# PSUM score tiles by half of a query tile, first loads over two queues, and more sigmoid groups, in a fused attention and feed-forward kernel

## The chip, the core and the metric

The kernel runs on one core of a Trainium2 chip. The metric is the time of one execution on the device, in microseconds (us). Each time is a median of three to nine executions of the same build.

The names in the profile are PE for TensorE's matmuls, PEld for its weight loads, DVE for VectorE, ACT for ScalarE, POOL for GpSimd and SP for the engine that issues most loads. L326 is line 326 of the kernel in question. Inserted lines shift the numbers, so the same instruction is L326 before, L335 after the change.

## The reference, cut to what matters

```python
# q, k, v: (8 batches, 8 heads, 576, 64); tau: scalar
scores = scale * np.matmul(q, k.transpose(0, 1, 3, 2))
thresh = np.max(scores, axis=-1, keepdims=True) - tau
scores = np.where(scores >= thresh, scores, -1000000000.0)
scores = scores - np.max(scores, axis=-1, keepdims=True)
attn = np.exp(scores)
attn = attn / (np.sum(attn, axis=-1, keepdims=True) + 1e-09)
attn_out = np.matmul(attn, v)
# x: attn_out as (4608, 512); w_gate, w_val: (512, 1536); w_out: (1536, 512)
g = x @ w_gate
silu = g * (1.0 / (1.0 + np.exp(-g)))
out = (silu * (x @ w_val)) @ w_out
```

## The kernel before: the parts that the argument touches

The order of instructions on each engine is fixed when the kernel is built. Attention for one batch is interleaved with the feed-forward products of the batch before it, which fill TensorE while the softmax goes through the other engines.

**A score block.** One block serves two heads and two half tiles of 64 queries each. It has 16 matmul calls, and each f32 call appears as two matmuls in the trace, so a full block reads as x32. Its result fills two PSUM tiles, and the pool has just two, so each block needs the tiles of the block before.

```python
ps_s = ctx.enter_context(tc.tile_pool(name="ps_s", bufs=2, space=bass.MemoryType.PSUM))
...
put = [(pss[h], u, h, q0 + u * D) for u in range(2) for h in range(2)] if t < NT else \
    [(pss[0], h, h, q0) for h in range(2)]
for x in range(0, len(put), 2):
    for g in range(NG):
        a, c = divmod(g, 2)
        for ps, u, h, col in put[x:x + 2]:          # two heads in turn: both PSUM tiles
            hs = heads[h]
            nc.tensor.matmul(ps[g * G:(g + 1) * G, u, 0:SH], qT[hs, col + a * G:col + (a + 1) * G],
                             kT[hs, c * SH:(c + 1) * SH], start=True, stop=True)   # L286
...
for x, tile_ in enumerate(pss):                     # one maximum for each PSUM tile, L306
    nc.vector.tensor_reduce(out=mx[:, 2 * x:2 * x + 2, 0], in_=tile_[:, :, 0:SH], axis=AX.X, op=ALU.max,
                            negate=True)
...
for x in range(m):                                  # four exponentials, L322
    nc.scalar.activation(ps[x], scs[x], AF.Exp, bias=nm[:, x:x + 1])
...
for x in range(m):                                  # four masking passes, L326; the last reader of the scores
    nc.vector.scalar_tensor_tensor(out=ps[x], in0=scs[x], scalar=th[:, x:x + 1], in1=ps[x],
                                   op0=ALU.is_ge, op1=ALU.mult, accum_out=sm[:, x, 0:1])
```

This is a ring: the scores free VectorE to take the maximum, then come exponentials and masking passes, and the masking passes free the PSUM tiles for the next block's scores. After the masking passes, ScalarE copies the row sums, VectorE takes their total and reciprocal, and GpSimd and ScalarE normalise the weights, which VectorE then transposes.

**First loads.** q and k go over SP's queue into one pair of places, so the second pair waits until the first is transposed; GpSimd scales q.

```python
raw = ld.tile([P, NJ, G], F32, name=f"{name}raw")
...
    nc.sync.dma_start(out=raw[g * G:(g + 1) * G], ...)                                    # L230
nc.gpsimd.tensor_scalar(out=raws[0], in0=raws[0], scalar1=scl, scalar2=None, op0=ALU.mult)  # L233
```

**Sigmoids.** ScalarE keeps the table of the exponential for attention, so sigmoids are collected in groups: a table load, the sigmoids, and a second load by a dummy exponential. The hidden tiles are then multiplied and, in most units, added up for a scheme with seven products instead of eight. A unit is a run of 256 tokens. Its last group takes three gate tiles, and at the last unit of a batch VectorE does its multiplications.

```python
def sigmoids(eng=None):
    eng = nc.vector if attended else eng or nc.gpsimd
    for hts, gt, own in unsig:
        nc.scalar.activation(gt, gt, AF.Sigmoid)                                          # L500
        for y, (x, ht) in enumerate(own):
            eng.tensor_tensor(out=ht, in0=ht, in1=gt[:, 2 * y:2 * y + 2, :], op=ALU.mult)   # L502
    if not attended:
        nc.scalar.activation(idle, tau_s, AF.Exp)                                         # L505
    ...                                             # three sums on eng for each pair, L513 to L515
...
if unsig:                                           # at the end of a unit
    sigmoids(nc.gpsimd if ready else nc.vector)
```

Of the kernel before, what the change touches and what calls it, by code (L numbers as in the profile page):

```python
# [10 lines left out]
F32 = mybir.dt.float32  # L11
U32 = mybir.dt.uint32
U64 = mybir.dt.uint64
AF = mybir.ActivationFunctionType
ALU = mybir.AluOpType
# [4 lines left out]
def kernel(  # L20
# [30 lines left out]
    nc = tc.nc  # L51
    P = 128
    B, H, S, D = q.shape
# [3 lines left out]
    NF = DFF // P  # L57
    G = 32
# [164 lines left out]
    def load_qk(i):  # L223
        b, hp_ = divmod(i, NP)
        raws = []
        for name, src, order in (("q", q, "(j r) (e d) -> e r j d"), ("k", k, "(j r) (e d) -> e r j d" if b == 0 else "(r j) (e d) -> e r j d")):
            raw = ld.tile([P, NJ, G], F32, name=f"{name}raw")
            for g in range(NG):
                h, e = divmod(g, 2)
                nc.sync.dma_start(out=raw[g * G:(g + 1) * G],  # L230
                                  in_=src[b, 2 * hp_ + h].rearrange(order, r=G, d=G)[e])
            raws.append(raw.rearrange("p j d -> p (j d)"))
        nc.gpsimd.tensor_scalar(out=raws[0], in0=raws[0], scalar1=scl, scalar2=None, op0=ALU.mult)  # L233
        return raws

    def load_v(seg):
# [29 lines left out]
    def scores(seg, t):  # L266
        qT, kT, tiles, halved = seg["qT"], seg["kT"], seg["tiles"], seg["halved"]
        if halved and "p" not in seg:
            seg["p"] = arenas[seg["i"] % 2]
        q0 = t * P - seg["q0"]  # L270
        heads = [slice(h * D, (h + 1) * D) for h in range(2)]
        if t < NT:
            pss = [ps_s.tile([P, 2, 512], F32, name="sc") for _ in range(2)]
            at = [t, NT + 1 + t]
        else:
            pss = [ps_s.tile([P, 2, 512], F32, name="sc")]
            at = [t]
        if halved:
            put = [(pss[h], u, h, q0 + u * D) for u in range(2) for h in range(2)] if t < NT else \
                [(pss[0], h, h, q0) for h in range(2)]  # L280
            for x in range(0, len(put), 2):
                for g in range(NG):
                    a, c = divmod(g, 2)
                    for ps, u, h, col in put[x:x + 2]:
                        hs = heads[h]
                        nc.tensor.matmul(ps[g * G:(g + 1) * G, u, 0:SH], qT[hs, col + a * G:col + (a + 1) * G],  # L286
                                         kT[hs, c * SH:(c + 1) * SH], start=True, stop=True)
        elif t < NT:
            for h, hs in enumerate(heads):
                for n in range(2):  # L290
                    nc.tensor.matmul(pss[h][:, n, 0:SH], qT[hs, q0:q0 + P], kT[hs, n * SH:(n + 1) * SH],
                                     start=True, stop=True)
        else:
            for n, h in ((0, 0), (1, 1), (1, 0), (0, 1)):
                hs = heads[h]
                nc.tensor.matmul(pss[0][hs, n, 0:SH], qT[hs, q0:q0 + D], kT[hs, n * SH:(n + 1) * SH],
                                 start=True, stop=True)
        mx, nm, th, ri = (stp.tile([P, 4, 2] if x == "mx" else [P, 4], F32, name=x) for x in ("mx", "nm", "th", "ri"))
        sm = sums[0]
        sums.rotate(1)  # L300
        if halved:
            m = 2 * len(at)
            scs = [ps[:, u, 0:SH] for ps in pss for u in range(2)]
            ps = [seg["p"][:, x, u * SH:(u + 1) * SH] for x in at for u in range(2)]
            for x, tile_ in enumerate(pss):
                nc.vector.tensor_reduce(out=mx[:, 2 * x:2 * x + 2, 0], in_=tile_[:, :, 0:SH], axis=AX.X, op=ALU.max,  # L306
                                        negate=True)
            meet(mx, m, largest)
            nc.vector.tensor_reduce(out=nm[:, 0:m], in_=mx[:, 0:m, :], axis=AX.X, op=ALU.min)  # L309
        else:  # L310
            m = len(at)
            scs = [ps[:, :, 0:SH] for ps in pss]
            ps = [pbufs[0][:, x, :].rearrange("p (n s) -> p n s", n=2) for x in range(m)]
            pbufs.rotate(1)
            for x in range(m):
                nc.vector.tensor_reduce(out=nm[:, x:x + 1], in_=scs[x], axis=AX.XY, op=ALU.max, negate=True)
        if halved:
            nc.scalar.activation(th[:, 0:m], nm[:, 0:m], AF.Identity, bias=cut, scale=-1.0)  # L318
        for x in range(m):
            if not halved:  # L320
                nc.scalar.activation(th[:, x:x + 1], nm[:, x:x + 1], AF.Identity, bias=cut, scale=-1.0)
            nc.scalar.activation(ps[x], scs[x], AF.Exp, bias=nm[:, x:x + 1])  # L322
        yield
        turn(1)
        for x in range(m):
            nc.vector.scalar_tensor_tensor(out=ps[x], in0=scs[x], scalar=th[:, x:x + 1], in1=ps[x],  # L326
                                           op0=ALU.is_ge, op1=ALU.mult, accum_out=sm[:, x, 0:1])
        tot = stp.tile([P, 4], F32, name="tot")
        if halved:
            yield  # L330
            meet(sm, m, same)
            yield
            nc.vector.tensor_reduce(out=tot[:, 0:m], in_=sm[:, 0:m, :], axis=AX.X, op=ALU.add)
        else:
            nc.vector.tensor_reduce(out=tot[:, 0:m], in_=sm[:, 0:m, 0:3:2], axis=AX.X, op=ALU.add)  # L335
        nc.vector.reciprocal(out=ri[:, 0:m], in_=tot[:, 0:m])  # L336
        if not halved:
            yield
        for x in range(m):
            if halved and not split and x % 2:  # L340
                nc.gpsimd.tensor_scalar(out=ps[x], in0=ps[x], scalar1=ri[:, x:x + 1], scalar2=None, op0=ALU.mult)  # L341
            else:
                nc.scalar.activation(ps[x], ps[x], AF.Copy, scale=ri[:, x:x + 1])  # L343
        if halved:
            unturned.append([seg["p"][:, x, :] for x in at])
        else:
            unflipped.append((seg, t, [p.rearrange("p n s -> p (n s)") for p in ps]))
            yield
        yield
# [144 lines left out]
            del xts[j]  # L494
        yield HCOST

    def sigmoids(eng=None):
        eng = nc.vector if attended else eng or nc.gpsimd
        for hts, gt, own in unsig:
            nc.scalar.activation(gt, gt, AF.Sigmoid)  # L500
            for y, (x, ht) in enumerate(own):
# [5 lines that stand above are left out]
            for x, ht in own:  # L507
                if hts["seven"] and x >= NF2 // 2:

                    x -= NF2 // 2  # L510
                    fs = slice(2 * x, 2 * x + 2)
                    h11, h21 = hts[x][:, :, 0:P], hts[x][:, :, P:2 * P]
                    eng.tensor_tensor(out=hs3[:, fs], in0=h11, in1=h21, op=ALU.subtract)  # L513
                    eng.tensor_tensor(out=h21, in0=h21, in1=ht[:, :, P:2 * P], op=ALU.add)
                    eng.tensor_tensor(out=hs2[:, fs], in0=h21, in1=h11, op=ALU.subtract)  # L515
        unsig.clear()
# [118 lines left out]
    def block():  # L635
        late, last = iter(()), None
        while True:
            if not ready:
                yield from late
                if not ready:  # L640
                    yield 0
                continue
            unit = ready.popleft()
            j, lo, hi = unit
            cs = slice(lo, hi)
            hts, gts = {"seven": unit not in (FIRST, SECOND)}, {}
            hidden[unit] = hts
            sums = sums_of_weights() if last == SECOND else iter(())
            for f in range(0, NF, GR):
                if f == EARLY:  # L650
                    yield from late
                yield from gate(j, cs, f, hts, gts)
                if f >= EARLY:
                    next(sums, 0)
                yield from value(j, cs, f, hts, gts)
            if unsig:

                sigmoids(nc.gpsimd if ready else nc.vector)
            late = outputs(unit)
            last = unit  # L660

# [101 lines left out]

    fetch_qk(0)
    prepare(segs[0])
    fetch_weights(1)
    fetch_qk(1)
    fetch_weights(1)
    load_v(segs[0])
    fetch_weights(2)  # L770
    prev = None
# [89 lines left out]
```

## Time and profile before

The time is 1612.3 us, the median of three runs (1610.49 to 1613.5). The profiled execution spans 1607.7 us.

| engine | busy us | share |
|---|---|---|
| TensorE | 1523.9 | 95% |
| VectorE | 1071.2 | 67% |
| ScalarE | 826.0 | 51% |
| GpSimd | 628.9 | 39% |

TensorE is the bound. Two groups of the page show the ring of waits between it and VectorE. The columns are line, engine, operation, output and input, sizes and count; then busy us and mean ns; then the idle time just before such instructions, and the releaser of most of it.

```profile
L286 PE MATMUL sc<-kT,qT 64*32 64x288 f32 x4032 | 181.5, 419 | 40.6 <-DVE pall L326 40.2
L306 DVE TENSOR_REDUCE mx<-sc 128x2 f32<-128x576 f32 x252 | 179.1, 748 | 46.2 <-PE sc L286 42.5
```

TensorE waits for VectorE's masking pass, and VectorE waits for TensorE's scores. A block's second matmul already writes the second PSUM tile, which comes free only with the fourth pass, and no tile is whole until the block's last matmuls.

### The profile page before, as it was taken

Reading aid. Unit: us, or ns where it says so; the run is one execution under the profiler, and the core shown is the slowest. Engines: PE = TensorE matmul, PEld = TensorE weight load, DVE = VectorE, ACT = ScalarE, POOL = GpSimd, SP = SyncE. Lnnn points to the kernel's source line nnn. Section 1 sums busy time; section 2 is a strip of 40 time slices with the busy share of each in tenths; the row PEclk is TensorE's granted clock in tenths of the full one; section 3 lists DMA queues with packets and bytes.
Section 4 is the critical chain, followed back from the end, with each engine's and each line's share of the span. In section 5 each row is a group of like instructions: output and inputs, shape, how many; then the busy total and the mean of one; then the engine's idle time right before and its main releaser. Section 6 shows DMA issues by size and latency. Waiting matters only on the chain.

```text
span 1607.7 us, 31245 instructions
## 1 busy us (share of the span) xinstructions
PE 1523.9 (95%) x11728; PEld 1145.3 (71%) x11728; DVE 1071.2 (67%) x3232; ACT 826.0 (51%) x2133; POOL 628.9 (39%) x613
## 2 busy tenths in 40 slices
PE   6999778899998999899999999999999999999998
PEld 4666554457676777677777777776777777788887
DVE  6887887777677777674777776767676777722212
ACT  5877656555554564544464646464556455611110
POOL 3555533327533253234344444445363535210010
PEclk9999899999999999999999999999999999999999
DMA  7541321111111111110211111101111110000000
GB/s 172 148 139 60 70 49 31 43 44 31 31 43 44 31 31 43 31 28 17 43 31 44 31 44 31 27 18 44 31 37 37 44 31 28 3 14 0 13 14 14
DMA packets 176422, 66.90 MB, mean 42 GB/s; under 512 B 159632, under 2 KB 159632, under 8 KB 176272
## 3 DMA queue, kind: packets, MB, share of 16 engines
q1 hardware_dynamic: 173328, 55.47, 15.6%
q0 software_dynamic: 2944, 9.44, 1.7%
q8 instruction: 93, 1.52, 0.4%
q14 instruction: 57, 0.47, 0.1%
HBM read 55.44 MB, written 9.44 MB: 40 GB/s over the span
## 4 chain that ended last, share of the span: by engine, by line
PE 77%; DVE 12%; ACT 6%; issue 2%; SPq 1%; POOL 1%; DMA 1%; DVEq 0%; POOLq 0%; ACTq 0%
PE pv L466 20%; PE pg L466 19%; PE po L575 18%; PE sc L286 9%; PE xa L423 8%; DVE pall L326 3%; DVE mx L306 2%; PE po L542 2%; DVE pall L356 2%; ACT pall L322 1%; DVE mx L261 1%; ACT gt L500 1%; ACT L500 1%; SPq L230 1%; ACT L505 1%
## 5 line engine op out<-in xcount | busy, mean ns | idle before, releaser
L466 PE MATMUL pv<-xall,wgv 128*128 128x256 f32 x1728 | 404.6, 385 | 1.9 <-ACT gt L482 1.9
L466 PE MATMUL pg<-xall,wgv 128*128 128x256 f32 x1728 | 403.1, 385 | 0.5 <-DVE xall L403 0.5
L466 PEld LDWEIGHTS pv<-xall,wgv 128*128 128x128 f32 x1728 | 327.7, 192 | 68.5 <-issue 21.2
L466 PEld LDWEIGHTS pg<-xall,wgv 128*128 128x128 f32 x1728 | 325.6, 191 | 69.1 <-issue 17.2
L341 POOL TENSOR_SCALAR pall<-pall,ri 128x288 f32<-128x288 f32 x243 | 241.0, 1002 | 320.2 <-DVE ri L336 279.0
L326 DVE SCALAR_TENSOR_TENSOR pall<-sc,th,pall 128x288 f32<-128x288 f32 (+1 forms) x540 | 258.0, 528 | 45.0 <-ACT pall L322 44.2
L322 ACT ACTIVATE pall<-sc,nm 128x288 f32<-128x288 f32 (+1 forms) x540 | 236.7, 511 | 0.6
L286 PE MATMUL sc<-kT,qT 64*32 64x288 f32 x4032 | 181.5, 419 | 40.6 <-DVE pall L326 40.2
L306 DVE TENSOR_REDUCE mx<-sc 128x2 f32<-128x576 f32 x252 | 179.1, 748 | 46.2 <-PE sc L286 42.5
L343 ACT ACTIVATE pall<-pall,ri 128x288 f32<-128x288 f32 (+1 forms) x297 | 152.9, 560 | 92.0 <-DVE ri L336 91.0
L356 DVE STREAM_TRANSPOSE pall<-pall 128x576 f32<-128x576 f32 x252 | 181.4, 754 | 3.3 <-POOL pall L341 3.3
L264 ACT COPY sums<-sums 32x4 f32<-32x4 f32 (+1 forms) x560 | 108.5, 194 | 139.3 <-DVE pall L326 129.8
L575 PE MATMUL po<-wo,ht 128*128 128x256 f32 x768 | 176.6, 382 | 0.0
L318 ACT ACTIVATE th<-nm,cut 128x4 f32<-128x4 f32 (+1 forms) x140 | 41.4, 296 | 248.0 <-DVE nm L309 248.0
L575 PEld LDWEIGHTS po<-wo,ht 128*128 128x128 f32 x768 | 144.8, 190 | 27.9 <-issue 4.6
L286 PEld LDWEIGHTS sc<-kT,qT 64*32 64x32 f32 x4032 | 72.1, 107 | 125.7 <-issue 101.8
L489 DVE TENSOR_TENSOR ht<-gt,pv 128x512 f32<-128x512 f32 x102 | 69.8, 684 | 135.4 <-PE pv L466 120.1
L502 POOL TENSOR_TENSOR ht<-ht,gt 128x512 f32<-128x512 f32 x72 | 89.6, 1271 | 167.2 <-ACT gt L500 167.2
L423 PE MATMUL xa<-pall,vall 64*64 64x288 f32 x2016 | 131.9, 410 | 6.7 <-issue 6.7
L423 PEld LDWEIGHTS xa<-pall,vall 64*64 64x64 f32 x2016 | 80.9, 135 | 53.7 <-issue 14.2
L588 POOL TENSOR_TENSOR ht<-ht,xall 128x256 f32<-128x256 f32 x48 | 34.8, 727 | 211.1 <-PE po L575 208.3
L482 ACT COPY gt<-pg 128x512 f32<-128x512 f32 x108 | 63.5, 588 | 79.2 <-PE pg L466 78.5
(100 smaller groups left out, 1482.3 us busy)
## 6 DMA issues: line engine op xcount, KB each, us to landing
vall<-in_v_dram SPq DMA_DIRECT2D x112, 144.0 KB, 3.4
qraw<-in_q_dram SPq DMA_DIRECT2D x128, 72.0 KB, 2.5
kraw<-in_k_dram SPq DMA_DIRECT2D x128, 72.0 KB, 2.9
out_dram<-ob POOLq DMA_DIRECT2D x32, 256.0 KB, 2.5
wo<-in_moe_w_gate_dram SPq DMA_DIRECT2D x16, 384.0 KB, 3.6
wo<-in_moe_w_val_dram SPq DMA_DIRECT2D x16, 384.0 KB, 4.1
xall<-in_moe_w_out_dram SPq DMA_DIRECT2D x6, 768.0 KB, 4.6
wo<-in_moe_w_out_dram SPq DMA_DIRECT2D x2, 768.0 KB, 4.4
```

Source lines behind the costliest of these rows:

```text
L264: nc.scalar.copy(out, in_[:, :, 0])
L286: nc.tensor.matmul(ps[g * G:(g + 1) * G, u, 0:SH], qT[hs, col + a * G:col + (a + 1) * G], kT[hs, c * SH:(c + 1) * SH], start=True, stop=True)
L306: nc.vector.tensor_reduce(out=mx[:, 2 * x:2 * x + 2, 0], in_=tile_[:, :, 0:SH], axis=AX.X, op=ALU.max, negate=True)
L322: nc.scalar.activation(ps[x], scs[x], AF.Exp, bias=nm[:, x:x + 1])
L326: nc.vector.scalar_tensor_tensor(out=ps[x], in0=scs[x], scalar=th[:, x:x + 1], in1=ps[x], op0=ALU.is_ge, op1=ALU.mult, accum_out=sm[:, x, ...
L341: nc.gpsimd.tensor_scalar(out=ps[x], in0=ps[x], scalar1=ri[:, x:x + 1], scalar2=None, op0=ALU.mult)
L343: nc.scalar.activation(ps[x], ps[x], AF.Copy, scale=ri[:, x:x + 1])
L356: nc.vector.transpose(out=p, in_=p)
L423: nc.tensor.matmul(xa[a][h * D:(h + 1) * D, at:at + n * G].rearrange("d (i q) -> d i q", q=G), vr[rs, h, j, :], p[rs, lo:lo + n, j, :], st ...
L466: nc.tensor.matmul(ps[:, i], wgv[:, mat, c, (f + i) * P:(f + i + 1) * P], x[:, c, cs], start=(c == 0), stop=(c == NCC - 1))
L502: eng.tensor_tensor(out=ht, in0=ht, in1=gt[:, 2 * y:2 * y + 2, :], op=ALU.mult)
L575: nc.tensor.matmul(ps, h(f), w[:, f, :], start=(f == 0), stop=(f == NF2 - 1))
```

## The change

The change has three parts, with the intent read from the code.

1. A PSUM tile holds one half of the query tile for both heads, instead of one head for both halves. The first half of a block's matmuls then needs one PSUM tile only, and the first maximum needs only those matmuls.
2. The second and third pair of q and k get places of their own. For the first two pairs k goes over ScalarE's queue, and ScalarE scales q. The aim is an earlier start.
3. In a batch's last unit an extra sigmoid group is formed before the last step, so that the last group is smaller. VectorE no longer does the multiplications there: GpSimd does, until attention is over. The aim is a shorter wait of the output products.

```diff
@@ load_qk @@
+        free = {1: 0, 2: 1}.get(i)
-            raw = ld.tile([P, NJ, G], F32, name=f"{name}raw")
+            if free is None:
+                raw = ld.tile([P, NJ, G], F32, name=f"{name}raw")
+            else:
+                n = 2 * free + len(raws)
+                raw = extra[:, n * S:(n + 1) * S].rearrange("p (j d) -> p j d", d=G)
+            queue = nc.scalar if i < 2 and name == "k" else nc.sync
-                nc.sync.dma_start(out=raw[g * G:(g + 1) * G],
+                queue.dma_start(out=raw[g * G:(g + 1) * G],
...
-        nc.gpsimd.tensor_scalar(out=raws[0], in0=raws[0], scalar1=scl, scalar2=None, op0=ALU.mult)
+        if i < 2:
+            nc.scalar.activation(raws[0], raws[0], AF.Copy, scale=scl)
+        else:
+            nc.gpsimd.tensor_scalar(out=raws[0], in0=raws[0], scalar1=scl, scalar2=None, op0=ALU.mult)
@@ scores @@
-            put = [(pss[h], u, h, q0 + u * D) for u in range(2) for h in range(2)] if t < NT else \
-                [(pss[0], h, h, q0) for h in range(2)]
+            put = [(pss[u], h, q0 + u * D) for u in range(len(pss)) for h in range(2)]
...
-                        nc.tensor.matmul(ps[g * G:(g + 1) * G, u, 0:SH], ...
+                        nc.tensor.matmul(ps[g * G:(g + 1) * G, h, 0:SH], ...
...
-            scs = [ps[:, u, 0:SH] for ps in pss for u in range(2)]
-            ps = [seg["p"][:, x, u * SH:(u + 1) * SH] for x in at for u in range(2)]
+            scs = [ps[:, h, 0:SH] for ps in pss for h in range(2)]
+            ps = [seg["p"][:, x, u * SH:(u + 1) * SH] for u in range(2) for x in at]
@@ sigmoids, block @@
-    def sigmoids(eng=None):
-        eng = nc.vector if attended else eng or nc.gpsimd
+    def sigmoids():
+        eng = nc.vector if attended else nc.gpsimd
...
+                if not ready and f == NF - 2 * GR:
+                    sigmoids()
             if unsig:
-                sigmoids(nc.gpsimd if ready else nc.vector)
+                sigmoids()
@@ start @@ (the weights' first two fetches now stand together, after the second q and k)
```

More of the change, by code (lines that the diff above doesn't have):

```diff
@@ L283, in scores @@
                     a, c = divmod(g, 2)
-                    for ps, u, h, col in put[x:x + 2]:
+                    for ps, h, col in put[x:x + 2]:
                         hs = heads[h]
-                        nc.tensor.matmul(ps[g * G:(g + 1) * G, u, 0:SH], qT[hs, col + a * G:col + (a + 1) * G],
+                        nc.tensor.matmul(ps[g * G:(g + 1) * G, h, 0:SH], qT[hs, col + a * G:col + (a + 1) * G],
                                          kT[hs, c * SH:(c + 1) * SH], start=True, stop=True)
@@ L765 @@
     prepare(segs[0])
-    fetch_weights(1)
     fetch_qk(1)
-    fetch_weights(1)
+    fetch_weights(2)
     load_v(segs[0])
```

## The prediction

> **What bounds the kernel now.** I read the page's busy shares and slices first, then the chain of waits (who waited for whom), then the timeline at the places where the largest waits lie, and last the order of instructions of both builds on each engine.
>
> ```profile
> span 1607.7 us, 31245 instructions
> PE 1523.9 (95%) x11728; PEld 1145.3 (71%) x11728; DVE 1071.2 (67%) x3232; ACT 826.0 (51%) x2133; POOL 628.9 (39%) x613
> ...
> PE   6999778899998999899999999999999999999998
> PEld 4666554457676777677777777776777777788887
> DVE  6887887777677777674777776767676777722212
> ```
>
> The reader is to see that TensorE (PE) is the bound of the last three quarters, and that its slack lies early: the first six slices (0 to 240 us) have PE at six to nine tenths with VectorE (DVE) at six to eight. PE is idle 1607.7 - 1523.9 = 83.8 us in all. Nothing that shortens another engine's work can give more than that, plus what waits hide inside PE's busy time and what half clock costs. The waits say which idle time the change aims at:
>
> ```profile
> DVE mx L306 <- PE sc L286: 42.5, 59, 2.9
> ...
> PE sc L286 <- DVE pall L326: 40.2, 31, 6.2
> ...
> PE po L575 <- DVE ht L502: 9.1, 2, 4.7
> ```
>
> (columns: us in total, times, longest). The score matmuls (sc, L286) wait for the masking pass of the tile before (pall, L326), because that pass holds the two PSUM tiles they write; the row maximum (mx, L306) waits for the score matmuls. By windows, 27.6 us of the 40.2 lie between 240 and 1400 us, 12.6 us before 240 us, where DVE also joins the weights (L195 to L201, about 3 us a tile) and is itself the limit.
>
> A third kind of loss is not in these sums. An undisturbed block of 32 score matmuls takes 1.20 us; this is one that is disturbed, in the timeline around 707 us:
>
> ```profile
> 707.43 0.51 DVE L326 SCALAR_TENSOR_TENSOR pall<-sc,th,pall 128x288 f32<-128x288 f32 x1
> 707.76 0.13 PEld L286 LDWEIGHTS sc<-kT,qT 64*32 64x32 f32 x2 [0.33 <-issue]
> 707.76 1.53 PE L286 MATMUL sc<-kT,qT 64*32 64x288 f32 x32
> 707.87 0.08 DVE L326 DVE_READ_ACCUMULATOR pall<-sc,th,pall 128x1 f32 x1
> ...
> 708.06 0.69 PEld L286 LDWEIGHTS sc<-kT,qT 64*32 64x32 f32 x30 [0.16 <-issue]
> ```
>
> The first matmul (head 0, first PSUM tile) starts, the next (head 1, second PSUM tile) stands until the fourth masking pass has ended at 707.95. PE counts as busy for all of 1.53 us, since matmuls overlap, but 0.33 us of it is a wait.
>
> **What the Trainium skill says.** Perfetto Trace Analysis, "Matmuls", says that independent matmul groups should rotate through PSUM banks so that the emptying of one overlaps the next group's matmuls; the trace shows the opposite here, each group needs both tiles at its second matmul. TensorE: Matmul & The Clock Gate, "What's actually happening", says that PE runs at half clock after an idle window of some 3.4 us and needs a busy one to recover; the trace agrees in kind (32 score matmuls at 417.47 us took 3.05 us instead of 1.20), though an idle stretch of only 1.88 us stood before them. ScalarE: Activation LUTs, "What ACT_TABLE_LOAD costs", gives about 1283 ns a load plus a drain; the loads here take 1.28 us, and a drain of its own does not show. DMA: Bandwidth & Descriptors, "Issuing engines are not separate DMA queues", says that issuing from two engines saves only issue time; the trace agrees that there is little else to save: from 3 to 7 us the DMA engines are busy 0.80 to 1.06 of the time at 127 to 159 GB/s.
>
> **Part 1, PSUM tiles by half of the query tile.** The order of instructions on PE is the same in both builds; only the tiles written, and so the waits, change. The first 16 matmuls now need only masking passes 1 and 2, and the first maximum needs only those 16.
> - Wait in the middle of a block. Passes 3 and 4 take about 0.44 us each, so they end up to 0.88 us after the first matmul may start, and 16 matmuls take 0.60 us. Per block, min(length - 1.20, 0.60) us is saved. I listed all 112 full blocks: 49 are longer than 1.3 us, and the capped sum is 3.3 us before 240 us, 2.9 us from 240 to 360, 6.1 us to 700, 8.6 us to 1400. The first does not count, because DVE is the limit there. The rest is 17.6 us; I take 14, since some will come back at the next wait.
> - Earlier maximum. Where DVE stands idle for the scores (42.5 us in 59 waits), it starts 0.60 us sooner, which brings the next masking pass forward. It matters only where the next block waits on it. About 12 us of waits ahead of full blocks remain after 240 us (for example 1.92 at 334, 2.48 at 594, 1.40 at 1008, 2.07 at 1090): an estimate of 4 us.
> - Half clock. Some spells of 3.4 us after such waits go. One costs up to half its length, 1.7 us; I count one or two: 2 us.
> Sum: -20 us.
>
> **Part 2, first loads.**
>
> ```profile
> 0.72 1.28 ACT L321 ACT_TABLE_LOAD   x1 [0.72 <-PEq L845]
> ...
> 5.54 1.73 POOL L233 TENSOR_SCALAR qraw<-qraw,scl 128x576 f32<-128x576 f32 x1 [4.24 <-DMA qraw<-in_q_dram]
> ...
> 7.42 0.78 DVE L748 STREAM_TRANSPOSE pall<-kraw 128x576 f32<-128x576 f32 x1 [3.40 <-DMA kraw<-in_k_dram]
> 8.13 0.40 DVE L749 STREAM_TRANSPOSE qT<-qraw 128x256 f32<-128x256 f32 x1
> ...
> 8.59 2.30 PE L291 MATMUL sc<-pall,qT 64*128 64x288 f32 x8 [8.59 <-DVE qT L749]
> ```
>
> PE starts at 8.59 us, when k has landed (7.42) and k and q are transposed. Both loads together are 8 x 72 KB, 590,000 bytes; at about 140 GB/s that is 4.2 us from 2.3 us on, so with two queues both land near 6.5 us (estimate), k 0.9 us sooner and q 1.0 us later than now. The scaling goes from POOL (1.73 us) to ScalarE (0.75 to 0.80 us, as L343 on 128x576). But in the new build ScalarE's table load stands behind the waits for q, not at 0.72 us: 6.5 + 1.28 + 0.80 = 8.6 us, then the transpose, so the first matmul is at about 9.0 us, 0.4 us later. The second pair of k and q, in places of its own, no longer makes DVE wait 0.74 us at 15.44; after that, DVE shows no wait on a load in the first 160 us. Net -0.3 us: nothing.
>
> **Part 3, sigmoids in more groups.** The order shows six more groups on ScalarE, each two loads and a dummy exponential, 2 x 1.28 + 0.20 = 2.76 us, or 16.6 us of ScalarE; the multiplications of four last groups also move from DVE (1.89 us for three, 9 x 0.43 for the sums) to POOL (about 1.27 us and 0.73 us each). What it aims at:
>
> ```profile
> 494.22 1.28 ACT L500 ACT_TABLE_LOAD   x1
> ...
> 495.52 1.67 ACT L500 ACTIVATE gt<-gt 128x512 f32<-128x512 f32 x3
> 496.18 1.89 DVE L502 TENSOR_TENSOR ht<-ht,gt 128x512 f32<-128x512 f32 x3 [0.90 <-ACT gt L500]
> ...
> 496.93 4.48 PE L575 MATMUL po<-extra,ht 128*128 128x256 f32 x12 [4.70 <-DVE ht L502]
> ```
>
> Two of the three tiles will be ready earlier, so 8 of the 12 matmuls run at once from 492.2 us; the other 4 wait for the last tile: load 1.28 + one sigmoid 0.63 + POOL 1.27 from 494.2 (or up to 2 us later, since the extra group delays ScalarE before it). They end at about 499 to 500 instead of 501.4 us: -1.7 us here, -1.2 us at the like place at 675 us. The last group is two sigmoids (1.05 us) shorter, which helps the waits at 193.68 (6.19 us) and 284.02 (5.09 us): -2 us. Against it, an extra group that stands ahead of the copies of the sums delays them by up to 2.76 us. After 680 us PE has work queued and hides that; of the others I take +2 us in all. Net: -3 us.
>
> Sum: -20 + 0 - 3 = -23 us, 1589 us; I round towards no gain, to 1591 us, because later waits are known to take up part of what an earlier one gives.
>
> **Rivals.** (a) DVE's chain is the real limit up to 700 us, and PE only waits in other places: then only the 8.6 us after 700 and a few more stay, about 1602 us. For it: DVE is busy 75 to 85% of 160 to 360 us. Against it: from 360 us on the chain that ended last is mostly PE. (b) The six groups are paid in full in new waits, as the old ones seem to be (a score wait of 0.3 to 2.5 us follows some 10 us after 406, 584, 992, 1079 and 1218 us): 6 x 1.5 = 9 us back, 1600 us. (c) Waits feed each other, so both halves of part 1 (1.2 us a stalled block) and several half-clock spells are saved in full: 30 to 35 us, 1579 us.
>
> **Range and chances.** (a) with (b) gives 1603, (c) a little under 1579; so 1578 to 1603 us. Faster by over 2% needs under 1580.1 us, which only (c) gives: 0.13. Slower by over 2% has no mechanism: 0.01.
>
> **What would show it.** Part 1 right: full score blocks of 1.4 to 1.6 us become 1.20 us; score waits on the masking pass fall from 40.2 us to 20 to 25 us, maximum waits on scores from 42.5 us to under 25 us. Part 2 right: ScalarE's first table load near 6.5 us and the first matmul within 0.5 us of 8.6. Part 3 right: the 12 matmuls near 497 and 675 us split into 8 and 4, with the wait between them of 3 to 5 us. I am wrong if PE's busy time does not fall by about 10 us, if PE waits in new places after the extra groups, or if the first matmul comes over 1 us sooner or later.

## The result, and the profile after

The changed kernel took 1599.3 us, the median of four runs (1598.65 to 1606.12), against 1611.39 us of four runs of the kernel before. The ratio is 0.9933 with a 95% interval of 0.9904 to 0.9962. Every ratio here is the mean time of one kernel's fast runs over that of the other's of the same rounds, so it is not quite the ratio of the medians quoted beside it. A repeat among the experiments gave 1599.05 us. So the change gains about 12 us (0.7%, under the 2% of the prediction's chances), within the range predicted, but little more than half of the 21 us forecast.

The page of the changed kernel:

```profile
span 1597.3 us, 31341 instructions
PE 1503.7 (94%) x11728; PEld 1131.2 (71%) x11728; DVE 1046.9 (66%) x3193; ACT 845.3 (53%) x2153; POOL 660.7 (41%) x650
...
L295 PE MATMUL sc<-kT,qT 64*32 64x288 f32 x4032 | 161.8, 417 | 37.3 <-DVE pall L335 35.6
L315 DVE TENSOR_REDUCE mx<-sc 128x2 f32<-128x576 f32 x252 | 177.8, 743 | 23.3 <-PE sc L295 22.1
```

PE's busy time fell by 1523.9 - 1503.7 = 20.2 us, nearly all of it in the score matmuls (181.5 to 161.8 us), although the same 4032 matmuls ran. ScalarE gained 19 us of work and GpSimd 32. VectorE's wait for scores halved, from 42.5 to 22.1 us, while TensorE's wait for the masking pass fell only from 40.2 to 35.6 us. Its busy time fell by 20.2 us and its span by only 10.4, so its idle time grew by 9.8 us. The chain of waits says where:

```profile
PE sc L295 <- DVE pall L335: 35.6, 18, 5.7
PE po L584 <- POOL ht L511: 15.1, 3, 6.5
PE sc L300 <- DVE qT L760: 10.5, 1, 10.5
```

The output products (po) now wait three times for GpSimd, 15.1 us, where they waited twice for VectorE, 9.1 us. The third, longest one (6.5 us) is new. The first matmul starts 1.9 us later (10.5 against 8.6 us).

**Where the time went.** Both builds run the same 11728 matmuls in the same order. So the start of matmul number n in one trace can be set against the start of the same matmul in the other, and the difference told along the span (after minus before):

| at (us of the kernel before) | start | 157 | 333 | 667 | 1000 | 1385 | end |
|---|---|---|---|---|---|---|---|
| changed kernel, us | +1.9 | +0.4 | -2.1 | -8.4 | -11.25 | -19.9 | -10.35 |
| the same kernel again (its execution of 1602.94 us) | +1.9 | +1.85 | +1.9 | -4.55 | -7.4 | -16.0 | -6.5 |

Some of each figure is the position of the matmuls around it. The second row is another execution of the same kernel: it falls 4 us behind up to 333 us and keeps that distance afterwards. So a difference of up to 4 us before 333 us, read from one trace of each kernel, may mean nothing. The shape is plain all the same: the change had gained 19.9 us by 1385 us and gave 9.5 us of it back at once.

**The gain.** This is the timeline of the changed kernel at the score block whose disturbed form the prediction shows (then at 707.76 us). The columns are start, duration, engine, line and operation.

```profile
698.35 0.52 DVE L335 SCALAR_TENSOR_TENSOR pall<-sc,th,pall 128x288 f32<-128x288 f32 x1
698.79 0.09 DVE L335 DVE_READ_ACCUMULATOR pall<-sc,th,pall 128x1 f32 x1
...
698.84 1.20 PE L295 MATMUL sc<-kT,qT 64*32 64x288 f32 x32
```

The block takes 1.20 us instead of 1.53. It hardly used its new right to start between the passes: the fourth pass ended at 698.87, 0.03 us after the block's start. Before, TensorE came some 0.2 us before the fourth pass had ended (707.76 against 707.94); here VectorE has all but caught up with it. Over all 112 full blocks, those longer than 1.3 us fell from 49 to 18, and their time above 1.20 us from 33.5 to 12.0 us.

**The loss.** The place at 1391 us is the last unit before attention ends. The timeline of the kernel before at that place:

```profile
1397.64 0.80 ACT L264 COPY sums<-sums 32x2 f32<-32x2 f32 x4 [1.12 <-DVE pall L326]
...
1398.93 1.00 POOL L341 TENSOR_SCALAR pall<-pall,ri 128x288 f32<-128x288 f32 x1 [2.93 <-DVE ri L336]
...
1400.75 0.65 DVE L489 TENSOR_TENSOR ht<-gt,pv 128x512 f32<-128x512 f32 x1
...
1401.59 1.90 DVE L502 TENSOR_TENSOR ht<-ht,gt 128x512 f32<-128x512 f32 x3 [0.19 <-ACT gt L500]
...
1403.01 1.24 PE L575 MATMUL po<-extra,ht 128*128 128x256 f32 x5
```

and of the changed kernel:

```profile
1376.67 1.28 ACT L509 ACT_TABLE_LOAD   x1
...
1377.96 1.15 ACT L509 ACTIVATE gt<-gt 128x512 f32<-128x512 f32 x2
...
1379.13 1.28 ACT L514 ACT_TABLE_LOAD   x1
...
1380.64 0.80 ACT L274 COPY sums<-sums 32x2 f32<-32x2 f32 x4
1381.13 0.72 POOL L522 TENSOR_TENSOR xall<-ht 128x256 f32<-128x256 f32 x1
1381.46 0.59 ACT L491 COPY gt<-pg 128x512 f32<-128x512 f32 x1
...
1385.73 1.00 POOL L350 TENSOR_SCALAR pall<-pall,ri 128x288 f32<-128x288 f32 x1
1386.77 0.78 DVE L365 STREAM_TRANSPOSE pall<-pall 128x576 f32<-128x576 f32 x1 [3.61 <-POOL pall L350]
1387.47 0.65 DVE L498 TENSOR_TENSOR ht<-gt,pv 128x512 f32<-128x512 f32 x1
...
1391.52 1.22 PE L584 MATMUL po<-extra,ht 128*128 128x256 f32 x2 [6.49 <-POOL ht L511]
```

The extra group (load, two sigmoids, load, dummy) stands on ScalarE ahead of the copies of the row sums, which could have started after the second masking pass had ended at 1377.7 and start at 1380.64, 2.9 us late. Their reciprocal is there at 1381.8, but GpSimd has six sums of the extra group first, 0.72 us each from 1381.13, so the normalisation starts at 1385.73, 3.9 us late. VectorE's queue has the transpose of those weights ahead of the last hidden product (L498), which needs nothing of them: its own inputs, the gate (gt, copied by L491) and the value product (pv), were ready at 1382.05. Only then follow table load, sigmoid, and a multiplication on GpSimd of 1.26 us. TensorE has stood for 6.49 us. The trace's clock record then has half clock from 1390.3 us for 6.8 us, 5.6 us of it after the wait, which costs about 3 us more. Before, no wait of TensorE stood here.

### The profile page after: what moved, and what is told of

Same layout as the page of the kernel before. It is cut to its first block, busy times and chain, and to the rows that moved or that the text cites.

```text
span 1597.3 us, 31341 instructions
## 1 busy us (share of the span) xinstructions
PE 1503.7 (94%) x11728; PEld 1131.2 (71%) x11728; DVE 1046.9 (66%) x3193; ACT 845.3 (53%) x2153; POOL 660.7 (41%) x650
## 5 line engine op out<-in xcount | busy, mean ns | idle before, releaser
L295 PE MATMUL sc<-kT,qT 64*32 64x288 f32 x4032 | 161.8, 417 | 37.3 <-DVE pall L335 35.6
L315 DVE TENSOR_REDUCE mx<-sc 128x2 f32<-128x576 f32 x252 | 177.8, 743 | 23.3 <-PE sc L295 22.1
L365 DVE STREAM_TRANSPOSE pall<-pall 128x576 f32<-128x576 f32 x252 | 181.5, 754 | 7.1 <-POOL pall L350 7.1
L511 POOL TENSOR_TENSOR ht<-ht,gt 128x512 f32<-128x512 f32 x84 | 104.8, 1274 | 191.0 <-ACT gt L509 191.0
L584 PE MATMUL po<-wo,ht 128*128 128x256 f32 x768 | 180.1, 388 | 0.0
L498 DVE TENSOR_TENSOR ht<-gt,pv 128x512 f32<-128x512 f32 x102 | 69.9, 685 | 141.2 <-PE pv L475 118.1
L295 PEld LDWEIGHTS sc<-kT,qT 64*32 64x32 f32 x4032 | 58.9, 106 | 116.9 <-issue 83.5
L491 ACT COPY gt<-pg 128x512 f32<-128x512 f32 x108 | 63.4, 587 | 79.0 <-PE pg L475 78.0
```

What stands on the lines that cost most here:

```text
L295: nc.tensor.matmul(ps[g * G:(g + 1) * G, h, 0:SH], qT[hs, col + a * G:col + (a + 1) * G], kT[hs, c * SH:(c + 1) * SH], start=True, stop=True)
L365: nc.vector.transpose(out=p, in_=p)
L584: nc.tensor.matmul(ps, h(f), w[:, f, :], start=(f == 0), stop=(f == NF2 - 1))
```

## The experiments

All eleven kernels gave correct results; each was timed in five rounds, against the kernel before on the same chip.

| kernel | median us | before, same rounds | ratio (95% interval) |
|---|---|---|---|
| part 1 alone | 1589.34 | 1611.63 | 0.986 (0.9847 to 0.9874) |
| part 2 alone | 1611.32 | 1611.63 | 0.9999 (0.9986 to 1.0011) |
| part 3 alone | 1621.74 | 1611.63 | 1.0065 (1.0052 to 1.0078) |
| part 1, late maximum | 1598.3 | 1611.63 | 0.9919 (0.9905 to 0.9933) |
| all but part 3 | 1591.08 | 1610.76 | 0.9879 (0.9865 to 0.9892) |
| all, extra groups on VectorE | 1607.21 | 1610.76 | 0.9974 (0.9961 to 0.9988) |
| all, no extra groups | 1595.72 | 1610.76 | 0.9906 (0.9892 to 0.9919) |
| all but part 3, table loaded early | 1590.37 | 1610.76 | 0.9874 (0.986 to 0.9887) |
| all, last place as before | 1589.37 | 1610.95 | 0.9864 (0.985 to 0.9877) |
| part 1, meant as late start | 1589.99 | 1610.95 | 0.987 (0.9857 to 0.9884) |
| all, again | 1599.05 | 1610.95 | 0.9922 (0.9909 to 0.9936) |

My theory was: part 1 gives somewhat over 20 us, part 2 nothing, and part 3 takes about 9 us back at one place. The rivals were that part 1 itself reaches its limit at VectorE (so that its own gain would be some 10 us), and that the six extra groups each cost a little.

### Each part alone

Part 1 alone is the kernel before with only the hunk "scores" of the diff above.

> Only the PSUM tiles by half of the query tile. My theory (the change gained 20 us up to 1385 us, nearly all of it from this part, and lost 9.5 us in one place at the end, which the sigmoid part made): 1590 to 1595 us, no TensorE gap at the end, full score blocks of 1.20 us. Rival (the sigmoid part made a good share of the 20 us, by taking work off VectorE): 1598 us or more.

It took 1589.34 us (1587.29 to 1589.66), 22 us less than before: as fast as any version, and faster than both kernels.

```profile
PE sc L285 <- DVE pall L325: 39.7, 19, 5.7
...
DVE mx L305 <- PE sc L285: 22.1, 18, 2.4
```

The named wait on the masking pass hardly moved (40.2 to 39.7 us), though the kernel gained 22 us. What went is inside busy time: blocks above 1.3 us fell from 49 to 17, their excess from 33.5 to 12.0 us. By matmul number, 20.9 of the 21.9 us gained from 157 us on lie inside the score blocks. The time at half clock after 20 us fell from 72.2 to 52.0 us in the profiled executions.

Part 2 alone has the hunks "load_qk" and "start", part 3 alone the hunk "sigmoids, block".

> Only the first loads. My theory: the first matmul comes 1.9 us later (10.5 us) as in the full change, and the time is the same as before within 2 us, since the weights' joins on VectorE set the pace afterwards. Rival: the 1.9 us go through to the end or grow: 1614 us or more.

Part 2 alone is worth nothing: 1611.32 us. Its first matmul came at 10.39 us, 1.8 us later than before, and the end shows no loss within the 2 us of the interval.

> Only the sigmoids in more groups, all on GpSimd. My theory: this part is a loss by itself, 3 to 9 us (1615 to 1621 us), most of it in one wait of TensorE on the last group of multiplications near 1400 us. Rival: without the PSUM part there is slack at the end and the wait does not arise: 1605 to 1610 us.

Part 3 alone costs 10 us: 1621.74 us, just above the range of my theory. Against the kernel before, its matmuls were 0.6 us late at 1390 us and 9.6 us late at 1410 us. Between them stands the same wait of 6.49 us for GpSimd. So the five earlier extra groups come to +0.6 us in sum, and the last to 9 us.

All but part 3 is the changed kernel with `sigmoids` as before.

> The full change without the sigmoid part (PSUM tiles and loads alone). My theory: 1588 to 1592 us, since the loads alone gave nothing and the PSUM part alone 1589 us, so the sigmoid part costs 10 us by itself and in the full change alike. Rival (the parts depend on each other; with the PSUM part the sigmoid part costs more or less than alone): outside 1586 to 1594 us.

It took 1591.08 us, 8 us under the changed kernel. The sum of the parts holds: -22 + 0 + 10 = -12 us, which is what the whole change gave.

### What in part 1 gives the gain

Part 1 lets TensorE start a block after two masking passes (early start), and lets VectorE take the first maximum after half a block (early maximum). One experiment takes away the second by taking the maximum of the later PSUM tile first:

```diff
-            for x, tile_ in enumerate(pss):
+            for x, tile_ in reversed(list(enumerate(pss))):
```

> The PSUM part alone, but the row maximum of the second tile is taken first, so that no maximum can start before the whole score block is done: it takes the earlier maximum away and leaves the earlier start of the score matmuls. If the wait in the middle of the block is most of the gain, as predicted (14 of 20 us): 3 to 6 us slower than the PSUM part alone. If the earlier maximum is most of it: 10 us or more slower, close to the kernel before.

It took 1598.3 us, 9 us more than part 1 whole, between the two ranges: 13 of the 22 us stay. VectorE's wait for scores went back to what it was before (59 waits), so the edit did what it should:

```profile
DVE mx L305 <- PE sc L285: 39.7, 59, 2.7
```

The other was to take away the early start by freeing the second PSUM tile first:

```diff
-        for x in range(m):
+        turns = [2, 3, 0, 1] if m == 4 else range(m)
+        for x in turns:
             nc.scalar.activation(ps[x], scs[x], AF.Exp, bias=nm[:, x:x + 1])
...
-        for x in range(m):
+        for x in turns:
             nc.vector.scalar_tensor_tensor(...)
```

> The PSUM part alone, but the exponentials and masking passes of a tile take the second PSUM tile first, so that the first 16 score matmuls of the next tile wait for all four masking passes: it takes the earlier start of the score matmuls away and leaves the earlier maximum. The late maximum cost 9 us of 22. If the two halves add up: 13 us slower than the PSUM part alone, about 1602 us. If they feed each other, so that each alone gives little: 1606 us or more. If the earlier maximum alone gives most: 1595 us or less.

It took 1589.99 us, the same as part 1 whole (ratios 0.987 and 0.986, intervals overlapping). That looks as if the early maximum alone gave everything, but the trace shows that the edit did not take the early start away:

```profile
416.23 0.52 DVE L326 SCALAR_TENSOR_TENSOR pall<-sc,th,pall 128x288 f32<-128x288 f32 x1
...
416.66 0.52 DVE L326 SCALAR_TENSOR_TENSOR pall<-sc,th,pall 128x288 f32<-128x288 f32 x1
416.86 0.21 PEld L285 LDWEIGHTS sc<-kT,qT 64*32 64x32 f32 x16 [2.17 <-issue]
416.89 1.50 PE L285 MATMUL sc<-kT,qT 64*32 64x288 f32 x32 [1.79 <-DVE pall L326]
...
417.10 0.52 DVE L326 SCALAR_TENSOR_TENSOR pall<-sc,th,pall 128x288 f32<-128x288 f32 x1
...
417.68 0.18 PEld L285 LDWEIGHTS sc<-kT,qT 64*32 64x32 f32 x16 [0.60 <-DVE pall L326]
```

These are the second, third and fourth pass of a block. The next block starts 0.14 us after the second has ended and 0.73 us before the fourth ends; only its second half (the other 16 weight loads) waits for the fourth. Eleven full blocks start like this, as many as in part 1 alone. So the first half wrote to the tile that the first two passes had freed, whichever that was; why the tiles changed places is not on record. The run repeats part 1 in another order, and no run shows what the early maximum gives alone. What is shown: the early start alone gives 13 us, and the early maximum adds 9 us to it.

How the early maximum does that is shown in part. VectorE's passes come earlier: of the 84 full blocks that follow a full block, 35 started over 0.1 us before the fourth pass had ended, in the kernel before and with the late maximum alike, and 13 in part 1 whole. By matmul number from 157 us on, against the kernel before, the early start alone (late maximum) gains 19.8 us inside the score blocks, but loses 4.2 us by longer waits ahead of them and 1.4 us at other products; part 1 whole gains 20.9 us inside them, loses 2.5 us ahead of them, and gains 2.9 us at other products. These figures hold different amounts of half clock (64.6 and 52.0 us after 20 us), so the split of the 9 us stays open.

### What in part 3 costs the time

Part 3 moves work from VectorE to GpSimd and splits the groups. Two builds separate these. In the first, the extra groups stay, but VectorE does the multiplications as before (`sigmoids(nc.vector)` for the extra group, `sigmoids(nc.gpsimd if ready else nc.vector)` for the last one). In the second, no extra group is formed, and only the move stays:

```diff
-                if not ready and f == NF - 2 * GR:
-                    sigmoids()
             if unsig:
                 sigmoids()
```

> The full change, but the multiplications and sums of the last groups stay on VectorE as before; the extra six groups of sigmoids on ScalarE remain. If the loss at the end comes from GpSimd (normalisations of scores queue behind the six sums there): no TensorE wait of over 3 us near 1390 us and 1586 to 1592 us. If it comes from the two extra table loads on ScalarE: the wait stays at 5 to 6.5 us and 1597 to 1600 us.

> The full change without the extra groups: the sigmoids of a last group stay together, but their multiplications and sums all go to GpSimd. If moving the work to GpSimd is what costs: a wait of TensorE of 3 to 7 us at all three places (near 490, 668, 1390 us), 1594 to 1600 us. If the extra groups cost: 1588 to 1592 us.

The split on VectorE took 1607.21 us, 16 us more than without part 3, which neither theory had expected. The loss is spread: 2.1 us more from 157 to 240 us, 3.0 to 360 (both within the spread of two executions), 3.8 to 700, 1.9 to 1385, and 5.0 after it, where a wait of 3.0 us stands. VectorE's wait for the sigmoids rose:

```profile
DVE ht L511 <- ACT gt L509: 26.2, 28, 2.3
```

It was 15.4 us in 22 waits without part 3. While VectorE stands there, the masking passes behind it stand too, and TensorE's scores wait for these. That this makes up the whole of the 16 us is argued, not shown. So GpSimd was the better engine for the extra groups' work.

The move alone took 1595.72 us, 4.6 us more than without part 3. Its waits of the output products on GpSimd are 5.0 us each at 493 and 669 us, where they were 4.4 us on VectorE, and a new one of 1.2 us at 1397. So most of the loss at the end comes with the extra group: it is 9.5 us with the group's sums on GpSimd, ahead of the normalisation, 5.0 us with them on VectorE, and 2.5 us with the move alone.

The last test of this undoes part 3 in that one place only:

```diff
+    NEAREND = unit_of("full", (B - 2) * NU + 1)
...
-                if not ready and f == NF - 2 * GR:
+                if not ready and f == NF - 2 * GR and unit != NEAREND:
                     sigmoids()
             if unsig:
-                sigmoids()
+                sigmoids(nc.vector if unit == NEAREND and not ready else nc.gpsimd)
```

> The full change, with the sigmoid part undone in the last place alone (the last groups before the end of attention, near 1380 us: one group of three, its multiplications and sums on VectorE); the other five places stay as in the full change. If the whole loss of the sigmoid part lies in that one place (9.5 us in the trace): 1588 to 1592 us, as without the sigmoid part. Rival, after the split on VectorE cost 16 us in many places: the other five places cost too and 1594 us or more.

It took 1589.37 us (1589.3 to 1589.81) beside 1599.05 us of the changed kernel in the same rounds: 9.7 us. Its matmuls run in step with those of the changed kernel until 1382 us. Then 9.5 us part them: about 6.5 us of wait and 3 us of half clock. The whole loss of part 3 is that place. This kernel and part 1 alone are equal within their intervals, so the five other extra groups and the loads are worth nothing that the intervals show, in sum. The simpler one, part 1 alone, is the version to keep.

> The full change as it is, again, because one of its four timed runs was 7 us above the other three, which makes its interval wide: 1598 to 1600 us if the fast three hold, 1602 us or more if the slow one is as common as the others.

It gave 1599.05 us (1598.52 to 1602.94), so the first result was not a matter of the chip.

### The start

> As the run without the sigmoid part, with a dummy exponential put ahead of the first scaling on ScalarE, so that the table is loaded while the loads are under way. The first matmul comes 1.3 us sooner (9.2 instead of 10.5 us), by my theory without any effect on the time over 1 us, since VectorE's joins absorb it. Rival: the start goes through to the end, 1.3 us or more.

The edit is to all but part 3, and brings the table load ahead of the wait for q:

```diff
+        if i == 0:
+            nc.scalar.activation(idle, tau_s, AF.Exp)
         if i < 2:
             nc.scalar.activation(raws[0], raws[0], AF.Copy, scale=scl)
```

The first matmul came at 9.11 us instead of about 10.4, and the time was 1590.37 us beside 1591.08: no difference that the intervals, some 2 us to either side, can show. So they cannot tell my theory from the rival of 1.3 us. That VectorE, which joins the weights in the first 150 us, absorbs a late start is argued, not shown: in the changed kernel the 1.9 us read 0.4 us at 157 us, in its second execution 1.85 us.

## Why the prediction was right or wrong

**Part 1, the sum: right (-20 us predicted, -22 measured).** The capped sums of 2.9, 6.1 and 8.6 us stand against measured gains of 1.5, 7.8 and 11.2 us in the same windows (part 1 alone). The sign "blocks of 1.4 to 1.6 us become 1.20" came true (49 blocks above 1.3 us became 17), and so did "maximum waits under 25 us" (22.1). The blocks that stood for both passes took 2.07 us and became 1.60: 0.48 us saved, not the cap of 0.60, since 16 matmuls alone take 0.72 us.

**Part 1, its terms: the first right, the second too small.** "Wait in the middle of a block" got 14 us, and the early start alone gave 13. "Earlier maximum" got 4 us and added 9. The step that failed is "It matters only where the next block waits on it". The waits ahead of full blocks after 240 us, on which this counted, hardly shrank: 10.2 us in the trace before, 11.0 with the late maximum, 9.9 in part 1 whole. The gain lies in other places, which the runs show only in part. That the sum of 14, 4 and 2 us came so close to 13 and 9 is partly luck.

**The sign on score waits: wrong.** I wrote 20 to 25 us; it was 35.6 us, and 39.7 us in part 1 alone, which gained most. The waits named in that view are the long ones ahead of blocks (5.7 us the longest), where VectorE's whole chain is late, and nearly none of those went. Those that went were hidden in busy time.

**Half clock: mis-sized at most.** I counted 2 us. In part 1 alone 20.2 us less ran at half clock, worth up to half of that, some 10 us. But the run meant as late start, which has both halves of part 1, kept 68.7 us at half clock in its profiled execution and was as fast in the median (that execution was its slowest, 1593.1 us). So spells differ between executions, and how much of the gain is theirs stays open. One reading was wrong: the block at 417.47 us (3.05 us instead of 1.20) does not show half clock alone. Eight blocks that stood for both passes took 2.07 us at full clock, so 0.87 us of the excess was the wait.

**Part 2: right in the time, wrong in the start.** Net nothing is what the run showed. The first matmul came at 10.5 us, not 9.0, so by my own sign ("over 1 us later") this step is wrong. The timeline of the changed kernel:

```profile
7.55 0.78 DVE L759 STREAM_TRANSPOSE pall<-kraw 128x576 f32<-128x576 f32 x1 [3.44 <-DMA qraw<-in_q_dram]
7.89 1.28 ACT L241 ACT_TABLE_LOAD   x1 [7.89 <-DMA extra<-in_q_dram]
...
9.18 0.77 ACT L241 ACTIVATE qraw<-qraw,scl 128x576 f32<-128x576 f32 x1
...
10.49 1.82 PE L300 MATMUL sc<-pall,qT 64*128 64x288 f32 x6 [10.49 <-DVE qT L760]
```

The table load stands behind the wait for q, and load and scaling take 1.28 and 0.77 us, as predicted. The step that failed is "with two queues both land near 6.5 us": k was usable at 7.55 and q at 7.89 us. The second q load, which has a place of its own now, was issued from 4.43 us on and shares the engines. By the windows of one microsecond, the DMA engines moved 205, 146, 144, 136 and 129 GB/s from 3 to 8 us, about 750,000 bytes between 3 and 7.89 us. By the trace's packets, 844,000 bytes had moved on the two queues by then, where the first pair has 590,000. Nearly all of the difference, some 250,000 bytes on SP's queue, is the second q load, which I had left out.

**Part 3: wrong (-3 us predicted, +10 measured alone).** The form at 492 and 669 us was as predicted: 8 matmuls at once, then waits of 3.75 and 4.88 us, then 4 matmuls. The gain at 492 us was 1.3 us by matmul number against the kernel without part 3 (predicted 1.7). At 669 us it was a loss of 1.3 us (predicted gain 1.2): the wait grew from 4.41 to 4.88 us, and the spell of half clock there was 6.8 us instead of 3.4. The two waits that a shorter last group was to help by 2 us fell as predicted in part 3 alone, from 6.19 to 5.14 us and from 5.09 to 4.05. The step that failed is "After 680 us PE has work queued and hides that". At the last place attention runs out, and TensorE's next products are those that need the group. I had seen the delay of the sums on ScalarE (2.76 us, measured 2.9), but not that GpSimd's six sums then delay the normalisation by 3.9 us more, nor that VectorE's hidden product stands behind the transposes. The sign "PE waits in new places after the extra groups" told this error. Here the Trainium skill could have helped: Perfetto Trace Analysis, "Tensor Engine Instruction (MATMUL, LD_WEIGHTS)", says that ScalarE, VectorE and GpSimd take their instructions strictly in order. The trace agrees: L498, with its inputs ready at 1382.05, ran at 1387.47 behind the transpose at 1386.77. GPSIMD Engine Reference, "4.1 Engine selection", puts GpSimd at about twice VectorE's time for two inputs; the trace has 1.26 us against 0.63 for a multiplication (1.90 for three) and 0.72 against 0.42 for a sum.

**The rivals.** Rival (b) named the time (1600 us), but not the cause: the groups were not paid 1.5 us each, five of the six cost nothing in sum. Rival (a) is refuted by part 1 alone, at 1589 us. Rival (c), 30 to 35 us, did not come. The upper end of the range does not follow from its own figures: (a) at 1602 us with the 9 us of (b) gives 1611, not 1603.

## What to carry to other kernels

In a ring of waits between two engines, an earlier hand-over at one end gave 13 us here and one at the other end 9 us more, nearly all of it hidden in busy time: look for such waits in the length of single blocks. An experiment that is to take one thing away shows nothing until its own trace shows that the thing is gone; here one run gave the time that a theory named, with the thing still in place. Before work is moved to an engine with time to spare or split into more groups, read what stands behind it in that engine's queue, above all at the place where the other work runs out. Parts of a change should be timed alone: here one part held all of the gain, and another gave half of it back in one place out of six.

## What the Trainium skill lacked or had wrong

- TensorE: Matmul & The Clock Gate, "What's actually happening", gives an idle window of some 3.4 us for half clock. In the kernel before, half clock followed a wait of only 1.88 us at 417.47 us (and 0.87 us in which the block behind it stood), while in the changed kernel a wait of 1.81 us at 415.50 us had no spell behind it. Spells in the clock record, but for one at the very end, are multiples of 3.4 us, which agrees with the page's free-running window; how short a wait can still bring a spell is not on the page.
- ScalarE: Activation LUTs, "What ACT_TABLE_LOAD costs", counts a drain of about 1380 ns with each switch of tables. Here a load took 1.28 us, the next activation began within 0.02 us of its end (1376.67 + 1.28, then 1377.96), and the load itself began 0.01 us after the activation before it.
- DMA: Bandwidth & Descriptors, "Issuing engines are not separate DMA queues", says that the queues' transfers interleave and what a second queue saves (time of issuing), but puts no number on what this can cost a transfer: with two queues and a second pair of loads in flight, q was ready at 7.89 us instead of 5.54, and k at 7.55 instead of 7.42.
- Perfetto Trace Analysis says that matmul ends are estimated and that matmul busy time is a bad measure, but no page says that a wait inside a block of small matmuls on several tiles counts as busy: a block of 1.20 us read as 1.53 us busy, and the changed kernel's busy time fell by 20.2 us with the same matmuls.
